# Sigmoid attention and a mixture of experts: three instructions put elsewhere in the loop over row blocks, two weight loads on another queue

## The chip, the cores and the metric

The kernel runs on one core of a Trainium2 chip. The metric is device time in microseconds (us), as the median of several runs. The core has a matrix engine (TensorE, PE in the profile; its weight loads are the row PEld), a vector engine (VectorE, DVE), a scalar engine (ScalarE, ACT), a general engine (GpSimd, POOL) and SyncE (SP), which here does little but start transfers. The engines run side by side, each through its own instructions in their order, and wait for each other by semaphores.

## What is computed

The reference, cut to what matters:

```python
# q, k, v: 8 batches x 12 heads x 448 positions x 64, float32
scores = q @ k^T / sqrt(64) - log(448)
attn = (1 / (1 + exp(-scores))) @ v
x = attn.transpose(0, 2, 1, 3).reshape(3584, 768)

# moe: w_skip 768, w_gate 768 x 8, w1 8 x 768 x 1024, w2 8 x 1024 x 768
out = x.copy()
do_compute = x @ w_skip > 0
xc = x[do_compute]
logits = xc @ w_gate
e_idx = argmax(logits)
gate_w = softmax(logits)[e_idx]
for e in range(8):                       # rows whose expert is e
    h = maximum(xc[e_idx == e] @ w1[e], 0)
    y[e_idx == e] = gate_w * (h @ w2[e])
out[do_compute] = xc + y
```

So a row either keeps its attention result, or gets a weighted two-layer network of one of eight experts added to it. Which rows go to which expert is known only once the attention is done.

## The kernel before

**Stages.** The attention runs over 48 pairs of heads and writes `x` to the output in memory. Beside it the rows are routed, and for each expert a list of records (row number and gate weight) is written to `lst`. Behind it stand two blocks of 128 rows of the expert with most rows, written out by hand, and then a loop over the blocks that are left, 14 in this run (L1565 and following). Each turn of that loop handles the rows of one block: gather them from memory, transpose them, multiply by the first weights (`ph`), apply the maximum and transpose (`pht`), multiply by the second weights (`py`), weigh the result, and add it to the rows in memory by a scatter.

**Exactness.** TensorE's fast float32 form (fp32r) keeps fewer bits, so each operand is split in two: a rounded high part `h` and the low part `l` that is left. Three products, high by high, high by low and low by high, give the result. For the weights these are `wh` and `wl` (from `raw`, the loaded weights), for the rows `xh` and `xl` (from `pxt`, the transposed rows), for the middle layer `hh` and `hl` (from `pht`).

**Four arms.** A table `slots`, worked out on the chip, says which kind each turn is. `block(i, False)` is a full block of 128 rows. `block(i, True)` is the splitting arm: a full block, the last for one expert's `wh` and `wl`, in which the next expert's `raw` weights are split into them as the products let go of them. `half(i)` and `few(i)` handle up to 64 and up to 32 rows of an expert straight from `raw`, in plain float32, and load the next expert's weights into `raw`. Every engine has the four arms in its program and jumps to the one that the table names, so a wait at the head of an arm must hold whichever arm ran before it; waits across arms are for counts that all arms make equal.

**What sets the order.** In an arm the order on each engine is that in which the code is written (`manual_schedule`). Ahead of the loop it is written too, but a scheduler may place instructions of the stretch up to L1257.

**Records.** `recs` holds three records for each partition: [0] the current block's, [1] the next one's, [2] the one after. `rn` is where GpSimd gathers the record after that. `advance()` (L1333 to L1339) moves [1] and [2] to [0] and [1] by way of `sv`, and casts the new [0]'s row number to the integer `rid`; with one piece for the splitting arm (one copy each way) and two for the others. `take_rec()` copies `rn` into [2] (L1343), at the head of the half and few arms and behind the first `hl` in the full and splitting ones.

**GpSimd in a block.** `fetch()` (L1280 and following) reads the next block's row numbers (`ri`, `rp[1]`), gathers its rows into `xn` (L564) and its record into `rn` (L414). `put()` (L1306 and following) reads the current block's row numbers from `rid` into `rp[0]` (L1308), looks at the weighed rows `ys` so that they are seen as done (`jk`), and scatters them with an addition (L574). In the splitting arm two of the eight low parts of the second weights, `wl2[6]` and `wl2[7]`, are subtracted on GpSimd (L1396), between `fetch()` and `put()`; two are done by VectorE ahead of the weighing and four behind `advance()`.

**Loads ahead of the loop.** The loop's first turn needs `raw` weights: first weights in four parts (`load_w1`) and second weights in four parts (`load_w2`). SyncE issues the four first parts and the second parts 0 and 1; all but the very first of these stand behind a wait for `done`, the last matmul of the blocks written out by hand. ScalarE issues the second parts 2 and 3, behind its own work on the first transposed rows (`xf`).

Of the kernel before, what the change touches and what calls it, by code (L numbers as in the profile page):

```python
# [15 lines left out]
ALU = mybir.AluOpType  # L16
# [7 lines left out]
def kernel(  # L24
# [11 lines left out]
    nc = tc.nc  # L36
# [3 lines left out]
    NE, _, FF = w1.shape  # L40
# [9 lines left out]
    NK2 = FF // P  # L50
# [51 lines left out]
    recs = const.tile([P, 3, REC], F32, name="recs")  # L102
    rn = const.tile([P, REC], F32, name="rn")
    nc.vector.memset(rn, 0.0)
    rid = const.tile([P, 3], I32, name="rid")
# [10 lines left out]
    wh2 = [wts.tile([P, DM], F32R, name=f"wh2_{i}") for i in range(NK2)]  # L116
    wl2 = [wts.tile([P, DM], F32R, name=f"wl2_{i}") for i in range(NK2)]
# [371 lines left out]
    def turn_x(x, h, px):  # L489
        for j in range(3):  # L490
            i = 3 * h + j
            nc.tensor.transpose(  # L492
                px[:, j * P : (j + 1) * P], x[:, i * P : (i + 1) * P], ident
            )
# [13 lines left out]
    def gemm1(h, part, xh, xl, ph, lag=False):  # L508

        kinds = ((xh, wh1), (xh, wl1), (xl, wh1))  # L510
        t = [(2 * j + 3 * (n == 2) if lag else 2 * n * NK1, n, j) for n in range(3) for j in range(NK1)]
        t.sort()
        for n in part:
            _, kind, j = t[n]
            a, w = kinds[kind]
            nc.tensor.matmul(  # L516
                ph[h],
                a[:, j * P : (j + 1) * P],
                w[j][h],
                start=(n == 0),  # L520
                stop=(n == len(t) - 1),
            )

    def relu(h, hs, ph):
        nc.scalar.activation(hs[:, h * H1 : (h + 1) * H1], ph[h], AF.Relu)  # L525

    def turn_h(h, hs, pt):
        for j in range(4):
            m = 4 * h + j
            nc.tensor.transpose(  # L530
                pt[:, j * P : (j + 1) * P], hs[:, m * P : (m + 1) * P], ident
            )

    def split_h(h, pt, hh, hl):
        nc.scalar.activation(hh[h], pt, AF.Copy)  # L535
        nc.vector.tensor_tensor(hl[h], pt, hh[h], op=ALU.subtract)  # L536

    def gemm2(j, hh, hl, py):
        h, m = divmod(j, 4)
        js = slice(m * P, (m + 1) * P)  # L540
        parts = [(n, o) for n in range(3) for o in range(2)]
        for n, o in parts:
            a, w = ((hh, wh2), (hh, wl2), (hl, wh2))[n]
            last = nc.tensor.matmul(  # L544
                half_y(py, o),
                a[h][:, js],
                w[j][:, o * H2 : (o + 1) * H2],
                start=(j == 0 and n == 0),
                stop=(j == NK2 - 1 and n == 2),
            )  # L550
        return last
# [493 lines left out]
    first_i = const.tile([P, 2], I32, name="first_i")  # L1045
# [48 lines left out]
    def whole_x(h, pieces):  # L1094
        for s in pieces:
            n = s.stop - s.start
            nc.scalar.activation(  # L1097
                xf[:, 3 * h + s.start : 3 * h + s.stop, :],
                pxt[h][:, s.start * P : s.stop * P].rearrange(
                    "p (j t) -> p j t", j=n  # L1100
                )[:, :, :MD],
                AF.Copy,
            )
# [98 lines left out]
    raw2 = [raw2g[j // 2][:, j % 2, :] for j in range(NK2)]  # L1202
# [15 lines left out]
            cond=nx[1],  # L1218
        )

    def load_w2(g, nx, queue=nc.sync):
        queue.dma_start(
            raw2g[g],
            w2[ds(nx[0], 1), g * 2 * P : (g + 1) * 2 * P, :].rearrange(
                "o (i p) f -> p (o i) f", p=P
            ),
            cond=nx[1],
        )

    def hi1(i, h):  # L1230
        nc.scalar.activation(wh1[i][h], raw1[i][h], AF.Copy)

    def lo1(i, h):
        nc.vector.tensor_tensor(wl1[i][h], raw1[i][h], wh1[i][h], op=ALU.subtract)

    def hi2(i):
        nc.scalar.activation(wh2[i], raw2[i], AF.Copy)

    def lo2(i):
        nc.vector.tensor_tensor(wl2[i], raw2[i], wh2[i], op=ALU.subtract)  # L1240

    dve, pool = nc.vector, nc.gpsimd
    ET = mybir.EngineType
    others = [e for e in mybir.ALL_ENGINES if e not in SP]
    kind_sp = nc.alloc_registers("kind", engines=SP)
# [2 lines left out]
    def look_ahead(col):  # L1248
        for reg, (j, most) in zip(
            (kind_sp, *names), ((TYP, SPLIT), (NXT, NE - 1), (HAS, 1))  # L1250
        ):
            nc.reg_mov(reg[ET.SP], entry(j, col, SP, most))

    def named():
# [4 lines left out]
    nx = (  # L1259
        nc.values_load(first_i[0:1, 1:2], engines=SP, min_val=0, max_val=NE - 1),  # L1260
        nc.values_load(first_i[0:1, 0:1], engines=SP, min_val=0, max_val=1),
    )

    nx_act = (
        nc.values_load(first_i[0:1, 1:2], engines=[ET.Activation], min_val=0, max_val=NE - 1),
        nc.values_load(first_i[0:1, 0:1], engines=[ET.Activation], min_val=0, max_val=1),
    )

    for n in range(4):
        load = load_w1(n % 2, n // 2, nx)  # L1270
        if n == 1:
# [5 lines left out]
            )  # L1277
        if n == 0:
            look_ahead(slice(2, 3))
    for g in range(4):  # L1280
        load_w2(g, nx if g < 2 else nx_act, nc.sync if g < 2 else nc.scalar)

    def fetch():


        pool.tensor_tensor(xn[:, 0:1], xn[:, 0:1], zf, op=ALU.add)
        pool.tensor_tensor(jk, rn[:, 0:2], rn[:, 0:2], op=ALU.add)
        pool.tensor_copy(ri, rn[:, 1:2])
        pool.tensor_tensor(rn[:, 0:1], rn[:, 0:1], zf, op=ALU.add)
        pool.tensor_tensor(rx, rix[:, 5:6], zero, op=ALU.add)  # L1290
        pool.tensor_tensor(rp[1], ri, zero, op=ALU.add)
        pool.tensor_tensor(rq, rp[1], zero, op=ALU.add)
        got = gather(xn, rp[1])

        tc.declare_no_dep(got.ins, group="put", across_iterations=True, reason="a token is in one block only")
        tc.add_to_no_dep_group("got", got.ins)
        gather_rec(rn, rx)
# [34 lines left out]
    def advance(pieces=2):  # L1332

        n = 2 // pieces
        for j in range(pieces):
            nc.vector.tensor_copy(sv[:, j * n : (j + 1) * n], recs[:, 1 + j * n : 1 + (j + 1) * n, 0:2])
        for j in range(pieces):
            nc.vector.tensor_copy(recs[:, j * n : (j + 1) * n, 0:2], sv[:, j * n : (j + 1) * n])
        nc.vector.tensor_copy(rid[:, 0:1], recs[:, 0, 1:2])  # L1339

    def take_rec():

        nc.vector.tensor_copy(recs[:, 2, 0:2], rn[:, 0:2])  # L1343

    def weigh_sum(y, p, gate):
        nc.vector.tensor_scalar(y, p, gate, None, op0=ALU.mult)

    def block(i, last):


        def split1(js, h):
            if last:
                for j in js:
                    hi1(j, h)
                for j in js:
                    lo1(j, h)

        look_ahead(ds(i + 3, 1))
        gemm1(0, range(G1), xh, xl, ph, last)
        relu(0, hs, ph)  # L1360
        split1(range(3), 0)
        gemm1(1, range(9), xh, xl, ph, last)
        turn_h(0, hs, pht[0])
        split_h(0, pht[0], hh, hl)
        take_rec()
        split1(range(3, NK1), 0)
        gemm1(1, range(9, G1), xh, xl, ph, last)
        relu(1, hs, ph)
        for h in range(2):
            turn_x(xn, h, pxt[h])  # L1370
        fetch()
        split1(range(3), 1)
        gemm2(0, hh, hl, py)
        turn_h(1, hs, pht[1])
        split_h(1, pht[1], hh, hl)
        split1(range(3, NK1), 1)
        if last:
            for h in range(2):
                whole_x(h, (slice(0, 3),))
            shift(dve)  # L1380
        else:
            ready_x()
        for j in range(1, NK2):
            gemm2(j, hh, hl, py)
        if last:
            for j in range(2):
                hi2(j)
            for h in range(2):
                hi_x(h, pxt[h], xh)
            for j in range(2, NK2 - 2):  # L1390
                hi2(j)
            for j in range(2):
                lo2(j)
            for j in range(NK2 - 2, NK2):
                dve.tensor_copy(wh2[j], raw2[j])
                pool.tensor_tensor(wl2[j], raw2[j], wh2[j], op=ALU.subtract)  # L1396
            for h in range(2):
                lo_x(h, pxt[h], xh, xl)
        else:
            shift(dve)  # L1400
        for o in range(2):
            rows = ys if last else yt
            weigh_sum(rows[:, o * H2 : (o + 1) * H2], half_y(py, o), recs[:, 0, 0:1])
        put(P, last)
        advance(1 if last else 2)
        if last:
            for j in range(2, NK2 - 2):
                lo2(j)

    def few(i):  # L1410

# [50 lines left out]
        for g in range(4):  # L1462
            load_w2(g, nx)
# [134 lines left out]
```

## Time and profile before

| what | value |
| --- | --- |
| time, median of 3 runs (lowest to highest) | 525.26 us (525.13 to 527.0) |
| the profiled execution's own time | 523.72 us |
| its span, first to last instruction | 521.8 us |
| granted TensorE clock, mean over the span | 0.992 of full speed |
| TensorE matmuls | 506.6 us busy, 97% of the span |
| VectorE | 298.0 us, 57% |
| ScalarE | 278.8 us, 53% |
| GpSimd | 266.6 us, 51% |
| loop over blocks | from 321.84 us of the span to its end |

The table is to be read so: times in the profile count from the start of the span, which is 1.9 us shorter than the execution's own time. An instruction's row in a timeline has its start, its length, its engine, the line, the operation with `output<-input`, the tile's shape, and in brackets how long the engine had waited ahead of it and for whom. "xN" at the end of a row stands for N such instructions one after another, with the length of all of them together.

### The profile page before, as it was taken

How to read it: one execution, taken by the hardware profiler on the slowest of the kernel's cores; microseconds unless marked ns; L12 is line 12 of the kernel's file. 1: busy time of each engine (PE TensorE's matmuls, PEld its weight loads, DVE VectorE, ACT ScalarE, POOL GpSimd, SP SyncE). 2: the span in 40 equal slices, each digit the busy share in tenths (PEclk: the TensorE clock that was granted, in tenths of full speed). 3: DMA queues.
4: the chain of work that ended last, by engine and by line, in shares of the span. 5: the costliest groups of instructions: out<-in, count | busy, mean ns of one | idle time of the engine just before them, and what ended most of it. 6: DMA issues, size and time to landing. Idle time of an engine off the chain costs nothing.

```text
span 521.8 us, 15390 instructions
## 1 busy us (share of the span) xinstructions
PE 506.6 (97%) x5033; PEld 341.5 (65%) x5034; DVE 298.0 (57%) x721; ACT 278.8 (53%) x481; POOL 266.6 (51%) x418
## 2 busy tenths in 40 slices
PE   8999999999999999999999999999999999999991
PEld 6875555545555446555455989948669797978790
DVE  4556856658668678587684952872223323249532
ACT  5776776767767667677674211942122323267221
POOL 4523553443557775766674332373333545456654
PEclk9999999999999999999999999999999999999996
DMA  8998887897989989999955017859393969696932
GB/s 210 214 248 187 174 178 160 171 179 174 202 187 239 234 193 206 206 217 219 197 117 119 11 42 241 336 169 360 98 355 139 329 234 346 237 348 214 361 121 47
DMA packets 140288, 107.21 MB, mean 205 GB/s; under 512 B 97099, under 2 KB 112731, under 8 KB 140240
## 3 DMA queue, kind: packets, MB, share of 16 engines
q1 hardware_dynamic: 133456, 96.09, 69.8%
q0 software_dynamic: 4576, 8.65, 6.9%
q10 hardware_dynamic: 2208, 1.83, 1.1%
q8 instruction: 30, 0.49, 0.4%
q14 instruction: 18, 0.15, 0.1%
HBM read 98.49 MB, written 17.56 MB: 222 GB/s over the span
## 4 chain that ended last, share of the span: by engine, by line
PE 95%; ACT 1%; DVE 1%; POOL 1%; issue 1%; DMA 1%; ACTq 0%; POOLq 0%; DVEq 0%
PE s L212 25%; PE pa L240 24%; PE py L544 11%; PE ph L516 11%; PE b_ph L516 3%; PE b_py L544 3%; PE py L1416 3%; PE ph L1416 3%; PE py L1485 2%; PE ph L1485 2%; PE pxt L492 2%; PE pl L280 2%; PE pht L530 1%; PE pg L297 1%; DMA kq_first<-in_q_dram 1%
## 5 line engine op out<-in xcount | busy, mean ns | idle before, releaser
L232 ACT ACTIVATE at<-s,bias 128x896 f32<-128x896 f32 (+1 forms) x191 | 173.8, 913 | 79.5 <-PE s L212 70.5
L212 PE MATMUL s<-x 64*64 64x448 f32 (+1 forms) x1528 | 170.2, 496 | 0.7 <-DVE x L194 0.7
L240 PE MATMUL pa<-at,v 64*64 64x448 f32 (+1 forms) x1536 | 168.5, 490 | 0.0
L176 POOL COPY kq<-kq 32x896 f32<-32x896 f32 (+1 forms) x96 | 87.7, 913 | 92.3 <-DMA kq<-in_q_dram 56.3
L212 PEld LDWEIGHTS s<-x 64*64 64x64 f32 x1528 | 83.9, 191 | 49.1 <-issue 25.2
L240 PEld LDWEIGHTS pa<-at,v 64*64 64x64 f32 x1536 | 65.6, 133 | 55.0 <-issue 45.7
L194 DVE STREAM_TRANSPOSE x<-kq 128x448 f32<-128x448 f32 x94 | 81.0, 936 | 4.4 <-PE pa L240 4.4
L250 DVE TENSOR_TENSOR xt<-xt,pa 128x448 f32<-128x448 f32 x48 | 29.8, 620 | 52.6 <-ACT xt L673 52.6
L414 POOL DMA_INDIRECT lst<-rec,idx x32 | 31.7, 990 | 17.8 <-DVE xt L250 5.7
L486 POOL TENSOR_TENSOR wl<-wr,wh 128x384 fp32r<-128x384 f32 (+1 forms) x28 | 31.2, 1124 | 12.8 <-DVE wh L485 8.3
L255 DVE STREAM_TRANSPOSE y<-xt 128x448 f32<-128x448 f32 x48 | 31.0, 645 | 5.8 <-DMA out_dram<-y 4.4
L574 POOL DMA_INDIRECT out_dram<-ys,rp x15 | 23.5, 1570 | 16.6 <-issue 8.4
L525 ACT ACTIVATE hs<-ph 128x512 f32<-128x512 f32 x14 | 8.4, 597 | 42.8 <-PE ph L516 34.8
L544 PE MATMUL py<-wh,hh 128*128 128x384 f32 x112 | 29.9, 348 | 0.0
L544 PE MATMUL py<-wh,hl 128*128 128x384 f32 x112 | 28.9, 339 | 0.5 <-DVE hl L536 0.5
L544 PE MATMUL py<-wl,hh 128*128 128x384 f32 x112 | 28.7, 337 | 0.0
L502 DVE TENSOR_TENSOR xl<-pxt,xh 128x384 fp32r<-128x384 f32 x30 | 15.3, 552 | 21.3 <-ACT xf L1097 20.8
L516 PE MATMUL ph<-wl,xh 128*128 128x512 f32 x84 | 26.6, 403 | 0.0
L536 DVE TENSOR_TENSOR hl<-pht,hh 128x512 fp32r<-128x512 f32 x14 | 9.7, 690 | 29.6 <-ACT hh L535 28.2
L673 ACT ACTIVATE xt<-pa 128x448 f32<-128x448 f32 x48 | 25.7, 535 | 0.8 <-PE pa L240 0.8
L516 PE MATMUL ph<-wh,xh 128*128 128x512 f32 x84 | 25.7, 403 | 0.0
L516 PE MATMUL ph<-wh,xl 128*128 128x512 f32 x84 | 24.5, 396 | 0.0
(279 smaller groups left out, 686.8 us busy)
## 6 DMA issues: line engine op xcount, KB each, us to landing
raw<-in_moe_w_dram SPq DMA_DIRECT2D x62, 768.0 KB
v<-in_v_dram SPq DMA_DIRECT2D x48, 256.0 KB
out_dram<-y SPq DMA_DIRECT2D x192, 56.0 KB
kq<-in_k_dram SPq DMA_DIRECT2D x46, 224.0 KB
kq<-in_q_dram SPq DMA_DIRECT2D x46, 224.0 KB
wr<-in_moe_w_dram SPq DMA_DIRECT2D x12, 256.0 KB
wr<-in_moe_w_dram SPq DMA_DIRECT2D x16, 192.0 KB
lst<-fill SPq DMA_DIRECT2D x4, 464.0 KB
```

What stands on the lines that cost most here:

```text
L176: nc.gpsimd.tensor_copy(a[BT:, :, :, :BT], a[:BT, :, :, BT:])
L194: nc.vector.transpose(xs[:, n].rearrange("p (r j) -> p j r", j=NJ), t.rearrange("p (j d) -> p j d", d=D)[:, :, :BT],)
L212: nc.tensor.matmul(sc[m * D : (m + 1) * D, j, : qs.stop - qs.start], xs[r, 0, first::NR7], xs[r, 1, qs], start=True, stop=True,)
L232: nc.scalar.activation(at[:, :, :n], sc[:, :, :n], AF.Sigmoid, bias=bias, scale=SCALE)
L240: nc.tensor.matmul(pa[j * D : (j + 1) * D, r, qs], vt[rs, j, r + c if c < 3 else 3 * (1 - r), :], at[rs, j, : qs.stop - qs.start], start=( ...
L250: nc.vector.tensor_tensor(x, x, pa[:, 1, :S], op=ALU.add)
L255: nc.vector.transpose(y, xts[b][:, hp, :])
L414: put = nc.gpsimd.indirect_dma_start(out=lst[:, :], out_offset=bass.IndirectOffsetOnAxis(ap=idx[:, c : c + 1], axis=0), in_=rec[:, c, :], ...
L486: nc.gpsimd.tensor_tensor(lo, r, hi, op=ALU.subtract)
L516: nc.tensor.matmul(ph[h], a[:, j * P : (j + 1) * P], w[j][h], start=(n == 0), stop=(n == len(t) - 1),)
L544: last = nc.tensor.matmul(half_y(py, o), a[h][:, js], w[j][:, o * H2 : (o + 1) * H2], start=(j == 0 and n == 0), stop=(j == NK2 - 1 and n ...
L1416: nc.tensor.matmul(dst[g * SM : (g + 1) * SM, :n], a, w, start=(j == 0), stop=(j == most - 1), tile_position=(0, g * SM),)
```

## The change

Three edits.

1. The cast of the row number (`rid`) leaves `advance()`, at the end of a block, and goes to `take_rec()`, behind the take of the record. GpSimd's `rp<-rid` in `put()` thereby waits for VectorE's cast of the same block, and the cast for GpSimd's read in the block before.
2. In the splitting arm GpSimd's two subtractions of low parts go from ahead of `put()` to the end of the arm, behind `advance()`. `lo2` gets an engine as its argument.
3. Ahead of the loop the second weights' parts 2 and 3 are issued by SyncE instead of ScalarE, right behind the first load and ahead of the wait for `done`. ScalarE's registers for them (`nx_act`) go.

```diff
-    def load_w2(g, nx, queue=nc.sync):
-        queue.dma_start(
+    def load_w2(g, nx):
+        nc.sync.dma_start(
...
-    def lo2(i):
-        nc.vector.tensor_tensor(wl2[i], raw2[i], wh2[i], op=ALU.subtract)
-
     dve, pool = nc.vector, nc.gpsimd
+
+    def lo2(i, eng=dve):
+        eng.tensor_tensor(wl2[i], raw2[i], wh2[i], op=ALU.subtract)
+
...
-    nx_act = (
-        nc.values_load(first_i[0:1, 1:2], engines=[ET.Activation], min_val=0, max_val=NE - 1),
-        nc.values_load(first_i[0:1, 0:1], engines=[ET.Activation], min_val=0, max_val=1),
     )
...
         if n == 0:
             look_ahead(slice(2, 3))
-    for g in range(4):
-        load_w2(g, nx if g < 2 else nx_act, nc.sync if g < 2 else nc.scalar)
+            for g in range(2, 4):
+                load_w2(g, nx)
+    for g in range(2):
+        load_w2(g, nx)
...
         for j in range(pieces):
             nc.vector.tensor_copy(recs[:, j * n : (j + 1) * n, 0:2], sv[:, j * n : (j + 1) * n])
+
+    def take_rec():
+
+        nc.vector.tensor_copy(recs[:, 2, 0:2], rn[:, 0:2])
         nc.vector.tensor_copy(rid[:, 0:1], recs[:, 0, 1:2])
-
-    def take_rec():
-
-        nc.vector.tensor_copy(recs[:, 2, 0:2], rn[:, 0:2])
...
             for j in range(NK2 - 2, NK2):
                 dve.tensor_copy(wh2[j], raw2[j])
-                pool.tensor_tensor(wl2[j], raw2[j], wh2[j], op=ALU.subtract)
...
         put(P, last)
         advance(1 if last else 2)
         if last:
-            for j in range(2, NK2 - 2):
-                lo2(j)
+            for j in range(2, NK2):
+                lo2(j, dve if j < NK2 - 2 else pool)
```

**GpSimd, the splitting arm.** The rows below are GpSimd's instructions from the record gather of `fetch()` to the scatter of `put()`, before. A row has the line, the operation and `output<-input` with the shape; `wl_6` and `wl_7` are the low parts 6 and 7, `REGISTER_ALU` a register step that keeps a wait's count.

```order
L1115 DMA rn<-lst,rx 128x16
L1396 TENSOR_TENSOR wl_6_130<-raw_3_4371,wh_6_122 128x768
L1396 REGISTER_ALU
L1396 TENSOR_TENSOR wl_7_131<-raw_3_4371,wh_7_123 128x768
L1308 TENSOR_TENSOR rp_4354<-rid,zero 128x1
L1309 REGISTER_ALU
L1309 TENSOR_TENSOR rs<-rp_4354,zero 128x1
L1314 REGISTER_ALU
L1314 TENSOR_TENSOR jk<-ys 128x2
L574 DMA out_dram<-ys,rp_4354 3584x768
```

And of the changed kernel, from the read of the row numbers to the arm's end:

```order
L1306 TENSOR_TENSOR rp_4354<-rid,zero 128x1
L1307 REGISTER_ALU
L1307 TENSOR_TENSOR rs<-rp_4354,zero 128x1
L1312 REGISTER_ALU
L1312 TENSOR_TENSOR jk<-ys 128x2
L574 DMA out_dram<-ys,rp_4354 3584x768
L1242 REGISTER_ALU
L1242 TENSOR_TENSOR wl_6_130<-raw_3_4371,wh_6_122 128x768
L1242 REGISTER_ALU
L1242 TENSOR_TENSOR wl_7_131<-raw_3_4371,wh_7_123 128x768
```

The two subtractions stood ahead of the store and stand behind it now; what comes next on GpSimd is `fetch()` of the following turn.

**VectorE, from a block's end to the next one's head.** Before, the end of the few arm, with `advance()` and its cast (`ISA` is a wait by itself):

```order
L1336 COPY sv<-recs 128x2 x2
L1338 REGISTER_ALU
L1338 COPY recs<-sv 128x2
L1338 REGISTER_ALU
L1338 COPY recs<-sv 128x2
L1339 ISA
L1339 CAST rid<-recs 128x1
L1555 UNCONDITIONAL_BRANCH
```

And the difference in the splitting arm, behind its first `hl`:

```order
 L536 REGISTER_ALU
 L536 TENSOR_TENSOR hl_4352<-pht,hh_4349 128x512
-L1343 COPY recs<-rn 128x2
+L1340 COPY recs<-rn 128x2
+L1341 ISA
+L1341 CAST rid<-recs 128x1
 L1234 REGISTER_ALU
 L1234 TENSOR_TENSOR wl_3_0_110<-raw_0_1_4348,wh_3_0_98 128x512
```

The cast with its wait has left the end of the block and stands behind the take of the record, in the full and splitting arms thereby behind `hl`; what is queued behind it there is the fourth low part of the first weights.

**SyncE ahead of the loop.** Before, from the first weight load on (`raw_0_0` to `raw_1_1` are the first weights' parts, `raw_0` to `raw_3` the second's):

```order
L1213 DMA raw_0_0_4347<-in_moe_w_dram 128x3x512
L1213 ISA
L1213 DMA raw_0_1_4348<-in_moe_w_dram 128x3x512
L1213 ISA
L1213 DMA raw_1_0_4365<-in_moe_w_dram 128x3x512
L1213 ISA
L1213 DMA raw_1_1_4366<-in_moe_w_dram 128x3x512
L1222 ISA
L1222 DMA raw_0_4367<-in_moe_w_dram 128x2x768
L1222 ISA
L1222 DMA raw_1_4368<-in_moe_w_dram 128x2x768
```

And now, from the same load on:

```order
L1213 DMA raw_0_0_4347<-in_moe_w_dram 128x3x512
L1222 ISA
L1222 DMA raw_2_4370<-in_moe_w_dram 128x2x768
L1222 ISA
L1222 DMA raw_3_4371<-in_moe_w_dram 128x2x768
L1213 ISA
L1213 DMA raw_0_1_4348<-in_moe_w_dram 128x3x512
```

Second parts 2 and 3 have come to this queue, behind the first load and ahead of the wait in front of `raw_0_1`; the rest follows as before.

## What it does to the time: the prediction

> **What bounds the kernel now.** I read the page's first two parts, then the chain of waits in order of time over the loop, and at each place where that chain leaves TensorE the timeline around it.
>
> ```profile
> span 521.8 us, 15390 instructions
> PE 506.6 (97%) x5033; PEld 341.5 (65%) x5034; DVE 298.0 (57%) x721; ACT 278.8 (53%) x481; POOL 266.6 (51%) x418
> ```
>
> TensorE is busy for 506.6 of 521.8 us, so only its few gaps can be won. The chain (columns: start, length, what) shows where they lie.
>
> ```profile
> 321.84 6.46 PE ph L516 x27
> ...
> 340.36 5.30 PE ph L1485 x24
> ...
> 452.10 2.76 PE ph L1416 x96
> ...
> 458.65 6.49 PE ph L516 x27
> ...
> 469.53 0.62 PE py L544 x2
> ...
> 477.96 2.76 PE ph L1416 x96
> ...
> 482.51 3.00 PE py L1416 x32
> 485.51 6.50 PE ph L516 x27
> ```
>
> The loop's 14 blocks can be told from the lines: L516 opens a full or splitting block, L1485 a half, L1416 a block for few rows. The first splitting block runs from 321.84 to 340.36, 18.52 us without a gap; the second from 458.65 to 477.96, 19.31 us. So the second loses 0.79 us, around 469.5, where TensorE waits for VectorE's `hl`. A block for few rows takes 458.65 - 452.10 = 6.55 us; the one behind the second split takes 485.51 - 477.96 = 7.55 us. It loses 1.00 us before its `py`. These two are the only gaps in the loop that the change can close: 1.79 us together, 0.34% of the time.
>
> **The first gap, and the moved cast.** The timeline at the second split's start:
>
> ```profile
> 463.66 1.66 ACT L1231 ACTIVATE wh<-raw 128x512 fp32r<-128x512 f32 x3
> 464.70 0.15 DVE L1339 CAST rid<-recs 128x1 int32<-128x1 f32 x1 [3.58 <-POOL rp L1308]
> 466.85 1.90 DVE L1234 TENSOR_TENSOR wl<-raw,wh 128x512 fp32r<-128x512 f32 x3 [2.00 <-PE ph L516]
> ```
>
> At the end of the block for few rows VectorE stands for 3.58 us before the row number cast, because GpSimd has not yet read the old numbers (its `rp` waits for the previous store to land). Only then does VectorE turn to the next block, and its first subtraction begins at 466.85, though ScalarE's high parts are there from 464.3 on (463.66 and a third of 1.66). `hl` stands behind three such subtractions. With the cast behind the take of the record, in the next block and behind `hl`, VectorE can start some 2.5 us sooner. I take this gap as closed: -0.79. Bounds: 0 if ScalarE, not VectorE, set `hl`, and -0.79 since the first split has no gap. The cast itself is not saved: 14 casts of 0.15 us stand elsewhere. Its new wait is for the `rp` of the block before; queued behind it are VectorE's second `hl` or its `xl`. In the case shown `rp` is past by 464.7 and the take comes behind `hl`, so behind 468.7 today (466.85 + 1.90), and it is satisfied. `rp` in turn now waits for this block's cast, whole steps earlier. In all other blocks the wait that goes is hidden already, since the chain there is TensorE alone: 0.
>
> **The second gap, and the moved subtractions.** Around the second split's end:
>
> ```profile
> 478.61 3.61 POOL L1396 TENSOR_TENSOR wl<-raw,wh 128x768 fp32r<-128x768 f32 x2 [3.39 <-DVE wh L1395]
> 480.63 1.63 DVE L1336 COPY sv<-recs 128x4 f32<-128x4 f32 x1
> 482.29 0.17 DVE L1338 COPY recs<-sv 128x4 f32<-128x4 f32 x1
> 482.80 3.56 DVE L1240 TENSOR_TENSOR wl<-raw,wh 128x768 fp32r<-128x768 f32 x4
> 483.33 1.92 POOL L574 DMA_INDIRECT out_dram<-ys,rp  x1 [0.55 <-issue]
> 485.50 0.91 POOL L1287 TENSOR_TENSOR jk<-rn 128x2 f32<-128x2 f32 x1
> 488.07 1.08 POOL L564 DMA_INDIRECT xn<-out_dram,rp  x1 [0.74 <-PE ph L516]
> 494.38 0.82 PE L492 MATMUL pxt<-ident,xn 128*128 128x128 f32 x6
> ```
>
> The view names ScalarE's `xh` as what `py` waited for at 482.51. I don't believe it: in the block before that,
>
> ```profile
> 455.81 2.84 PE L1416 MATMUL py<-raw,ht 128*32 128x384 f32 x32
> 456.14 0.87 ACT L498 ACTIVATE xh<-pxt 128x384 fp32r<-128x384 f32 x2
> 456.86 0.18 POOL L1286 TENSOR_TENSOR xn<-xn,zf 128x1 f32<-128x1 f32 x1 [0.19 <-PE py L1416]
> 458.76 1.08 POOL L564 DMA_INDIRECT xn<-out_dram,rp  x1 [0.75 <-PE py L1416]
> ```
>
> `py` starts at 455.81, ahead of `xh` at 456.14. What ends just before 482.51 is VectorE's `recs<-sv` (482.29 + 0.17 = 482.46); TensorE's wait is a count of VectorE's instructions, common to all arms, and in the splitting arm it reaches to this copy. The copy is late because `sv` before it took 1.63 us, where the copy back of the same numbers takes 0.17. It ends at 482.26, when GpSimd's subtractions do (478.61 + 3.61 = 482.22). With them behind the store, the copy falls to about 0.17 and this gap closes as well: -1.00. Bounds: 0 if `xh` were the cause, and -1.00.
>
> **What is late next.** The two subtractions, 3.61 us, now stand on GpSimd's queue ahead of the next block's fetch, whose gather brings `xn` for the full block at 485.51. This gather took, from issue to landing:
>
> ```profile
> DMA to landing us min/median/max: 6.1/6.1/6.1
> ```
>
> So it lands at 488.07 + 6.1 = 494.2, and TensorE transposes `xn` at 494.38: today it is just in time. If TensorE comes 1.79 us sooner it is ready at 492.6, and the gather alone decides. Its new time: `sv` marks the end of the weighing, 480.63 - 0.79 = 479.84. The store follows after a probe of `ys`, priced as the 0.18 us operation of L1286, and 0.55 of issue as now, at 480.6, and with its 1.92 holds GpSimd to 482.5. Alone the subtractions would end at 486.1. But VectorE's four subtractions (0.89 us each) then run from about 480.5 (482.80 is 2.17 behind the start of `sv`; 1.46 of these go) to 484.1. The row of `jk` shows what meets there: 0.91 us at 485.50, up to 486.41, the end of VectorE's last one (482.80 + 3.56 = 486.36), for an operation like the 0.18 us one of L1286 at 456.86. So GpSimd's first subtraction waits for the running one to end, at 483.2, and runs to 485.0; VectorE's last goes in between, to 485.9; the second ends at 487.7. From there the fetch needs 458.76 - 456.86 = 1.90 us to its gather: 489.6, landing at 495.7, and TensorE starts 0.2 later: 495.9 against 494.38, **+1.5**. This replaces the -1.79; the two don't add, and a VectorE that is late with `xl` meanwhile hides under the same wait. Bounds: no meeting at all and a store of 1.41 us as in the last block (the row below) give 482.0, 485.6, 487.5, 493.6 and so -0.6; two full waits of 0.89 (487.9) and one more in the fetch (`jk` at 0.91 in place of 0.18: 2.63) give 490.5, 496.6 and +2.4.
>
> The Trainium skill, SBUF — State Buffer, Who interferes with whom, says that a VectorE instruction with two SBUF inputs contends with a GpSimd instruction that reads SBUF, and that whichever starts first holds the shared ports to its end. The rows show only the short GpSimd operation that waits; by this rule VectorE's subtraction also waits for a long one, which gives the +1.5, and without it the sum would be -0.1.
>
> Behind the first split the same delay is covered:
>
> ```profile
> 350.27 1.08 POOL L564 DMA_INDIRECT xn<-out_dram,rp  x1 [0.75 <-PE py L1485]
> DMA to landing us min/median/max: 6.8/6.8/6.8
> 361.46 0.82 PE L492 MATMUL pxt<-ident,xn 128*128 128x128 f32 x6
> ```
>
> It lands at 357.1 for a use at 361.46; 4.4 us of slack against at most 2.4, or 3.2 where TensorE gains no 0.79 as that split has no gap.
>
> **The loads ahead of the loop.**
>
> ```profile
> 312.82 1.00 POOL L564 DMA_INDIRECT xc<-out_dram,rid  x1 [0.30 <-issue]
> DMA to landing us min/median/max: 3.9/3.9/3.9
> 317.87 0.82 PE L492 MATMUL pxt<-ident,xc 128*128 128x128 f32 x6
> ```
>
> ScalarE issued the third and fourth second weights behind its work on these transposes; SyncE now does so right behind its first load, ahead of this gather, since what they wait for is past. Two weight loads then run beside the gather of `xc`, which today lands at 312.82 + 3.9 = 316.7, 1.15 us ahead of its use. Nothing is won in return: the first split has no gap. The gathers of `xn`, most of them beside such loads, give the price:
>
> ```profile
> DMA to landing us min/median/max: 3.4/5.4/6.8
> ```
>
> Unchanged it costs 0; at 6.8 it lands at 319.6, and with 0.2 to the start TensorE loses 319.8 - 317.87 = 1.95. I take the median, 5.4: 318.2, start 318.4, **+0.55**. The Trainium skill, DMA: Bandwidth & Descriptors, Queues, rings and completion order, says that each DMA engine takes turns between the queues that have work; by that the gather would get half the rate for its whole length, and the sum would stay near this; no run here shows it for `xc`. The two other loads of SyncE keep their place behind `done`, and what ScalarE saves in issues hid beside TensorE.
>
> **The tail.** The last store is on the chain:
>
> ```profile
> 515.66 1.41 POOL out_dram L574
> ```
>
> Its `rp` has one more wait, long satisfied, for a register step: below 0.05, and 0 in the sum.
>
> **Sum.** +1.5 + 0.55 = +2.05. The profiled execution took 523.72 us, 521.8 of it span; it would take 525.8. The median of the runs shown is 525.26, 1.54 above the profiled one, so I predict 525.26 + 2.05 = **527.3 us**.
>
> **Rivals.**
> - *The gains stay* (22%). GpSimd and VectorE don't meet and the gather lands in time; for it speaks that the store leaves nearly 3 us sooner, against it that 3.61 us stand before the fetch. From -1.79 with nothing late to -0.6 by the low bound above; at -0.6 524.7.
> - *The load holds back the first rows* (15%), slower beyond doubt: SyncE's two loads delay `xc` to a landing after 6.8 us, +1.95, and with +1.5 that is 528.7; with both upper ends, +4.35, 529.6. It decides as soon as `xc` takes over 317.87 - 0.2 - 312.82 = 4.85 us. For it speaks the load's place directly ahead, against it that a first load already ran beside the gather at 3.9.
> - *Nothing of it reaches TensorE* (8%): `hl` and `py` wait as before since ScalarE is the bound, and the gather comes no later: 525.3.
>
> My own case has the other 55%, with its range -0.1 to +3.5: 525.2 to 528.8.
>
> **How the numbers follow.** The range leaves out the part of the first rival below -0.9 and the top of the second: 524.4 to 529.4. A measurement of this kernel tells about 0.5% (2.6 us) from no change, so faster means below 522.6, which no bound reaches: 0.03 for what I don't see. Slower means above 527.9: nearly all of the second rival and some fifth of my own case, 0.25. The rest, 0.72, is the same.
>
> **What would show it.** In the changed kernel's timeline: the cast at the head of the blocks and no wait for `rp` at their ends; the second splitting block near 18.5 us and the block behind it near 6.55; `sv` there at 0.2 us; the two GpSimd subtractions behind the store, longer than 1.8 us each or with a gap; then the gather near 489.6 less the entry's shift, and TensorE idle before `pxt` in the following full block. At the entry, `xc` landing later than 3.9 us and a gap before its transposes. I am wrong if that gather is issued before 488, or lands in under 5 us, or if TensorE stands at `hl` or `py` as before.

## The result, and the profile after

The changed kernel takes 531.12 us (median of 6 runs, 529.31 to 532.26) against 525.19 us before (6 runs beside them, 524.62 to 527.0): a ratio of 1.0105, 95% interval 1.0088 to 1.0123. It is slower by 5.9 us, where 2.05 was forecast, and lies above the range. The profiled execution took 531.16 us.

The page's first two parts, after:

```profile
span 529.2 us, 15413 instructions
PE 510.3 (96%) x5033; PEld 343.6 (65%) x5034; DVE 302.6 (57%) x721; ACT 278.5 (53%) x481; POOL 270.6 (51%) x418
```

The span grew by 7.4 us, but TensorE is also *busy* for 3.7 us more with the same 5033 matmuls. Waits alone can't do that: some matmuls ran slower. The chain of waits, after (lines above L1250 have moved by two or three):

```profile
310.84 0.45 PE b_pht L814 x4
...
313.80 7.24 DMA xc<-out_dram,rid
321.08 0.88 PE pxt L492 x6
...
325.10 6.46 PE ph L516 x27
...
462.05 6.53 PE ph L516 x27
...
490.38 0.17 DVE wl L1242
...
491.25 0.16 DVE recs L1340
491.47 7.94 PE ph L516 x21
...
511.46 2.76 PE ph L1413 x96
```

and the row of the chain before that answers to the first:

```profile
309.85 0.44 PE b_pht L814 x4
```

Read by stages, each against the same stage before:
- Ahead of 310 us the changed kernel is 0.99 us later. That is the attention, whose length differs from run to run: in the profiles of this study its end (the first product of the blocks by hand) lies between 282.94 and 285.16, and the profile of before is the earliest of all. It is no part of the change.
- At the entry 325.10 - 321.84 = 3.26, less these 0.99: **+2.27**. The gather of `xc` takes 7.24 us from issue to landing, and is on the chain.
- Up to the second splitting block +0.14, in that block 18.52 in place of 19.31: **-0.79**. In the block for few rows behind it 6.55 in place of 7.55: **-1.00**. Both gaps have closed.
- In the full block behind that, from the start of its first product to that of the next block's, 24.28 in place of 18.56: **+5.72**. From there on nothing differs.

The timeline at that place shows what the chain's odd rows (VectorE's `wl`, then `recs`, then TensorE) mean:

```profile
480.57 2.83 PE L1413 MATMUL ph<-raw,xf 128*32 128x128 f32 x96
483.13 0.16 DVE L1334 COPY sv<-recs 128x4 f32<-128x4 f32 x1
483.52 7.80 DVE L1242 TENSOR_TENSOR wl<-raw,wh 128x768 fp32r<-128x768 f32 x4
485.44 4.20 POOL L1242 TENSOR_TENSOR wl<-raw,wh 128x768 fp32r<-128x768 f32 x2
487.12 1.66 PE L516 MATMUL ph<-wh,xh 128*128 128x512 f32 x6
489.76 1.59 POOL L1285 TENSOR_TENSOR jk<-rn 128x2 f32<-128x2 f32 x1
491.25 0.16 DVE L1340 COPY recs<-rn 128x2 f32<-128x2 f32 x1
491.46 2.93 PE L516 MATMUL ph<-wl,xh 128*128 128x512 f32 x6 [2.69 <-DVE rid L1341]
493.04 1.07 POOL L564 DMA_INDIRECT xn<-out_dram,rp  x1 [0.75 <-PE ph L516]
494.19 2.76 PE L516 MATMUL ph<-wh,xl 128*128 128x512 f32 x6
496.75 1.96 PE L516 MATMUL ph<-wh,xh 128*128 128x512 f32 x6
501.79 0.82 PE L492 MATMUL pxt<-ident,xn 128*128 128x128 f32 x6
```

`sv` takes 0.16 us, as foreseen. VectorE's four subtractions take 7.80 us, 3.56 before. Behind them on its queue stands the take of the record, and TensorE starts its first low-part product 0.05 us after that take (491.25 + 0.16 = 491.41), having stood for 2.69 us. Then three groups of six products take 2.93, 2.76 and 1.96 us, where 1.66 is the first group's and 1.56 the rule: about 3 us more.

How the 7.80 us are shared out, from the answer on the tile `wl` (duration in ns: least, median, most):

```profile
L1242 DVE TENSOR_TENSOR wl<-raw,wh x4: 945/956/5189, 483.5 to 490.4; 128x768 fp32r<-128x768 f32 x4
L1242 POOL TENSOR_TENSOR wl<-raw,wh x2: 2412/2413/2414, 485.4 to 487.2; 128x768 fp32r<-128x768 f32 x2
```

Three of VectorE's are as ever; the third took 5.19 us, from 485.27 to 490.46, and so ended 0.82 us, about the length of one alone, behind the end of GpSimd's second (485.44 + 4.20 = 489.64). The two engines do not take turns here. And the windows (length; busy time of PE, PEld, DVE, ACT, POOL; granted clock; DMA share; GB/s) show the slow products:

```profile
487.38:490.79 3.41, 1.40 (x6) 0.79 (x5) 3.41 (x2) 0.22 (x1) 3.41 (x5) 1.00 1.03 282
490.79:494.21 3.42, 2.75 (x7) 2.17 (x8) 3.25 (x12) 0.93 (x2) 2.41 (x7) 0.50 1.05 319
494.21:497.62 3.41, 3.41 (x10) 2.64 (x9) 0.24 (x3) 0.55 (x1) 2.75 (x8) 0.50 1.03 412
497.62:501.03 3.41, 3.41 (x18) 2.82 (x17) 0.42 (x1) 0.64 (x2) 1.41 (x1) 1.00 1.04 390
```

TensorE's granted clock was full up to 490.79, near the end of the idle time, half for 6.83 us from there, and full again from 497.62 on.

### The profile page after: what moved, and what is told of

Its sections match the earlier page's. It is cut to its first block, busy times and chain, and to the rows that moved or that the text cites. A ratio compares the mean times of both kernels' runs of the same rounds, so it can differ in the third digit from the quotient of the medians.

```text
span 529.2 us, 15413 instructions
## 1 busy us (share of the span) xinstructions
PE 510.3 (96%) x5033; PEld 343.6 (65%) x5034; DVE 302.6 (57%) x721; ACT 278.5 (53%) x481; POOL 270.6 (51%) x418
## 4 chain that ended last, share of the span: by engine, by line
PE 93%; issue 2%; DMA 1%; DVE 1%; POOL 1%; ACT 1%; DVEq 0%; POOLq 0%; ACTq 0%
PE s L212 25%; PE pa L240 24%; PE ph L516 12%; PE py L544 11%; PE b_ph L516 3%; PE b_py L544 2%; PE py L1413 2%; PE ph L1413 2%; PE py L1482 2%; PE ph L1482 2%; PE pxt L492 2%; PE pl L280 2%; DMA xc<-out_dram,rid 1%; PE pht L530 1%; PE idle L627 1%
## 5 line engine op out<-in xcount | busy, mean ns | idle before, releaser
L240 PEld LDWEIGHTS pa<-at,v 64*64 64x64 f32 x1536 | 67.0, 133 | 54.8 <-issue 47.7
L516 PE MATMUL ph<-wl,xh 128*128 128x512 f32 x84 | 27.9, 422 | 2.7 <-DVE rid L1341 2.7
L516 PE MATMUL ph<-wh,xl 128*128 128x512 f32 x84 | 25.7, 412 | 0.0
```

The costliest lines, as they stand in the source:

```text
L240: nc.tensor.matmul(pa[j * D : (j + 1) * D, r, qs], vt[rs, j, r + c if c < 3 else 3 * (1 - r), :], at[rs, j, : qs.stop - qs.start], start=( ...
L516: nc.tensor.matmul(ph[h], a[:, j * P : (j + 1) * P], w[j][h], start=(n == 0), stop=(n == len(t) - 1),)
```

## The experiments

All times are medians beside runs of the kernel before; the ratio's 95% interval is in brackets. The table has, for one profiled execution of each, three stretches of TensorE's work taken from the starts of its products: from the first product of the blocks by hand to the first transposes of `xc` (entry), the block for few rows ahead of the second split with that split (few + split), the block for few rows behind it (few), and the full block that follows.

| kernel | time, beside before | ratio | entry | few + split | few | full |
| --- | --- | --- | --- | --- | --- | --- |
| before | | | 34.94 | 25.86 | 7.55 | 18.56 |
| all three edits | 531.12, 525.19 | 1.0105 [1.0088, 1.0123] | 37.15 | 25.24 | 6.55 | 24.28 |
| e1_cast | 524.9, 525.36 | 0.9988 [0.9976, 1.0] | 34.97 | 25.22 | 7.39 | 18.52 |
| e2_subs | 528.46, 525.36 | 1.0064 [1.0043, 1.0084] | 34.95 | 25.65 | 6.55 | 22.17 |
| e3_loads | 527.88, 525.36 | 1.0055 [1.0035, 1.0074] | 36.99 | 25.84 | 7.53 | 18.52 |
| e4_no_loads | 528.12, 525.36 | 1.0046 [1.0029, 1.0063] | 34.94 | 25.22 | 6.55 | 22.90 |
| e5_subs_vector | 524.9, 525.32 | 0.9989 [0.9972, 1.0005] | 34.95 | 25.09 | 7.59 | 18.56 |
| e6_one_behind | 526.51, 525.32 | 1.0015 [0.9995, 1.0035] | 34.93 | 25.09 | 6.73 | 20.64 |
| e7_one_ahead | 525.76, 525.32 | 0.9999 [0.9982, 1.0016] | 34.97 | 25.13 | 8.21 | 18.56 |
| e8_one_load | 527.13, 525.32 | 1.0024 [1.0006, 1.0042] | 36.09 | 25.93 | 7.53 | 18.55 |
| e9_reduce | 524.7, 525.5 | 0.9983 [0.9966, 1.0] | 34.92 | 25.09 | 7.38 | 18.56 |
| e10_cast_again | 524.4, 525.5 | 0.9982 [0.9967, 0.9997] | 34.97 | 25.09 | 7.39 | 18.53 |
| e11_loads_behind | 525.45, 525.5 | 0.9996 [0.9981, 1.0011] | 34.96 | 25.36 | 7.52 | 18.54 |
| e12_all_again | 530.98, 525.19 | 1.0093 [1.0069, 1.0118] | 37.11 | 25.11 | 6.60 | 22.88 |

### Each edit by itself

The theory after the reading: three effects that add, one of each edit. The rivals: the loss belongs to another edit, or to the gather of `xn` as predicted.

**e1_cast**: the kernel before with the first edit (`rid` cast in `take_rec`).

> The cast alone. My theory: the second splitting block falls from 19.31 to about 18.6 us and the rest stays, so -0.7 us against the kernel before. Rival: the cast's new wait for GpSimd, with VectorE's next work queued behind it, is what costs time in the changed kernel; then this kernel is slower by some 3 to 6 us by itself, with TensorE idle in the full block behind the second split.

0.5 us faster at the edge of the interval, few + split 0.64 shorter, the full block unchanged. The cast's wait costs nothing; its rival falls.

**e2_subs**: the second edit (`lo2` on GpSimd behind `advance`).

> The moved subtractions alone. My theory: the block for few rows behind the second split falls by 1.0 us to 6.55; in the full block behind it VectorE's third low part is held for some 5 us beside GpSimd's two, the take of the record comes that much later, and TensorE idles about 2.7 us ahead of its first product with a low part; +1.7 us where TensorE's clock stays, up to +4.7 where it falls to half for some 6 us after the idle time. Rival (the step as predicted): the gather of xn decides, TensorE idles about 1.5 us before pxt and not before; +1.5 us at most. Rival of the cast: no loss here, -1.0 us.

+3.1 us. The timeline:

```profile
490.23 0.15 DVE L1344 COPY recs<-rn 128x2 f32<-128x2 f32 x1
490.44 1.67 PE L516 MATMUL ph<-wl,xh 128*128 128x512 f32 x6 [3.16 <-DVE recs L1344]
492.01 1.07 POOL L564 DMA_INDIRECT xn<-out_dram,rp  x1 [0.73 <-PE ph L516]
498.14 0.84 PE L492 MATMUL pxt<-ident,xn 128*128 128x128 f32 x6
```

There is no cast at this place in this kernel, and TensorE starts 0.06 us after the take all the same: so it is the take that it waits for, not the cast which the changed kernel's row names. The semaphore records of the trace fit: the product waits for VectorE's counter, and the take raises this counter by a number, where its neighbours count one. The product needs low parts of first weights, which only a splitting arm makes, so a block for few rows would give all of these counts at once, with its take; the counts themselves are not in the trace. In this execution the products keep 1.67 us (no fall of the clock), and the full block is 3.6 us longer: 3.3 at the take (the first low-part product starts 490.44 - 485.61 = 4.83 us into the block, 1.51 before) and the rest behind it, 0.16 of this at `pxt`, 6.13 us after the gather's issue. So there are two waits, one behind the other. The first is where TensorE stands; the second, the gather that I had predicted, still ends last by some 0.2 us and sets the sum where the clock holds.

**e3_loads**: the third edit.

> The two loads alone. My theory: the gather of xc lands about 7.2 us after its issue in place of 3.9, TensorE waits for it some 2.0 us ahead of the first transposes, and nothing is won elsewhere: +2.0 us. Rival: the longer gather of the changed kernel was one execution's chance, and the price is the 0.55 us that I predicted or nothing.

+2.5 us, and the wait stands where expected:

```profile
314.94 1.00 POOL L564 DMA_INDIRECT xc<-out_dram,rid  x1 [0.30 <-issue]
322.07 0.87 PE L492 MATMUL pxt<-ident,xc 128*128 128x128 f32 x6 [1.88 <-DMA xc<-out_dram,rid]
```

**e4_no_loads**: the first and second edit.

> Cast and subtractions together, loads as before. My theory: the three edits add: -0.7 -1.0 +2.7 and up to 3.0 more where the clock falls, so +1.0 to +4.0 us, and the entry as in the kernel before. Rival: loads and subtractions need each other (the loads' shift moves the meeting of VectorE and GpSimd), then this one is not slower than the kernel before.

+2.8 us. With e3's +2.5 that makes +5.3; all three together have +5.9, within the intervals. The edits add, and need nothing of each other.

### What holds VectorE

**e5_subs_vector**: the cast, and both subtractions on VectorE.

```diff
-                pool.tensor_tensor(wl2[j], raw2[j], wh2[j], op=ALU.subtract)
...
-            for j in range(2, NK2 - 2):
-                lo2(j)
+            for j in range(2, NK2):
+                lo2(j, dve)
```

> The cast, and both subtractions behind the store on VectorE instead of GpSimd; loads as before. My theory (GpSimd's two hold VectorE's third for 5.2 us): nothing is held any more; VectorE's six take 6 x 0.89 = 5.3 us in place of 7.8, the take comes about 2.4 us sooner than with GpSimd, and TensorE's 2.7 us of idle time in the full block shrink to about 0.3, with no fall of the clock; -1.6 + 0.3 = -1.3 us against the kernel before. Rival (VectorE is late simply because the block for few rows is 1 us shorter and the fetch comes behind): most of the loss stays, 0 to +1.

```profile
480.90 5.30 DVE L1242 TENSOR_TENSOR wl<-raw,wh 128x768 fp32r<-128x768 f32 x6
482.11 3.50 PE L1416 MATMUL py<-raw,ht 128*32 128x384 f32 x32 [0.31 <-ACT ht L1444]
486.12 0.16 DVE L1343 COPY recs<-rn 128x2 f32<-128x2 f32 x1
487.04 1.56 PE L516 MATMUL ph<-wl,xh 128*128 128x512 f32 x6
```

Six subtractions in 5.30 us, 0.88 each: without GpSimd beside them none is held, the take comes at 486.12, and the full block is back at 18.56. The main theory holds. The time is only 0.4 us below that of before, though, since the block for few rows lost again what it had won (7.59): its `py` takes 3.50 us. I had not expected this. TensorE's count for `py` is reckoned from the arm's end; with two more VectorE instructions there it no longer falls on the copy to `recs` but on the second of the six subtractions: in the trace TensorE's wait for VectorE's counter inside `py` ends at 482.77, 0.04 us behind the end of that subtraction.

**e6_one_behind**: one of the two on GpSimd behind the store, the other on VectorE.

> The cast, one subtraction behind the store on GpSimd and the other on VectorE; loads as before. My theory: VectorE's third is held for one GpSimd subtraction only, some 2.4 us less than for two, but VectorE has one more of 0.9 us: the take comes some 1 to 1.5 us sooner than with both on GpSimd, TensorE idles 1.2 to 2.0 us; between 0 and +0.5 us. Rival (VectorE and GpSimd alternate, so that a VectorE instruction waits for one GpSimd instruction at most): held about as long as with two, less than 2.5 us, and idle time much as now.

```profile
481.16 6.87 DVE L1242 TENSOR_TENSOR wl<-raw,wh 128x768 fp32r<-128x768 f32 x5
483.08 2.39 POOL L1242 TENSOR_TENSOR wl<-raw,wh 128x768 fp32r<-128x768 f32 x1
488.17 1.66 PE L516 MATMUL ph<-wl,xh 128*128 128x512 f32 x6 [1.56 <-DVE rid L1344]
489.74 1.07 POOL L564 DMA_INDIRECT xn<-out_dram,rp  x1 [0.74 <-PE ph L516]
495.93 0.84 PE L492 MATMUL pxt<-ident,xn 128*128 128x128 f32 x6
```

Five take 6.87, which is 2.4 more than 5 x 0.89; with two of GpSimd's the four took 4.2 more. One GpSimd subtraction holds VectorE for its length, two for both: turns would have given the same hold twice. The idle time is 1.56 as expected, and the gather is then late by another 0.2 us at `pxt`, 6.19 us after its issue. The stages of this execution add up to +0.5 (-0.77, -0.82 and +2.08), the top of what was expected. The median is +1.2, with an interval from -0.3 to +1.8 that holds +0.5; what the rest of it would be isn't shown.

**e7_one_ahead**: one of the two on GpSimd in the old place, the other on VectorE behind `advance`.

> The cast, one subtraction on GpSimd in its old place ahead of the store and the other on VectorE behind advance; loads as before. My theory: GpSimd is done before the copy to sv, so both gaps close (-0.6 and -1.0), and VectorE's five have nothing of GpSimd's beside them but the short ones of the fetch; the take comes ahead of TensorE's use; -1.5 us, TensorE's full block at 18.55. Rival: the copy is still held, by the one subtraction; then -0.6.

A miss: no change, and the block for few rows at 8.21.

```profile
479.17 1.83 POOL L1242 TENSOR_TENSOR wl<-raw,wh 128x768 fp32r<-128x768 f32 x1 [2.01 <-DVE wh L1396]
479.37 2.04 DVE L1396 CAST wh<-raw 128x768 fp32r<-128x768 f32 x1 [0.44 <-PE py L544]
483.12 0.84 PE L492 MATMUL pxt<-ident,xn 128*128 128x128 f32 x6 [0.77 <-DVE ys L1347]
```

GpSimd now starts between VectorE's two casts of `wh` and holds the second: 2.04 us for what takes 0.56. The hold was not removed but moved. By itself it doesn't give the 8.21: in e1_cast the second cast is held for 2.04 us too, and `ys` begins 3.00 us into the block for few rows, 3.01 here, yet that block takes 7.39. The difference is what TensorE waits for. In e1_cast its transposes wait for `xl` (0.24 us), here for `ys` (0.77), and `py` takes 3.54 in place of 3.00. As in e5_subs_vector, one more VectorE instruction at the arm's end shifts where TensorE's count falls; the trace's wait inside `py` ends 0.04 us behind the first of the five subtractions.

**e9_reduce**: the cast; the copies to `sv` and back as reductions, GpSimd's work where it was.

```diff
+        if pieces == 1:
+            V.tensor_reduce(sv, recs[:, 1:3, 0:2].unsqueeze(3), axis=AX.X, op=ALU.max)
+            V.tensor_reduce(recs[:, 0:2, 0:2], sv.unsqueeze(3), axis=AX.X, op=ALU.max)
+            return
```

> The cast; GpSimd's two subtractions in their old place ahead of the store; in the splitting arm the copies to sv and back to recs become reductions over an axis of length one on the same engine. My theory: what holds the copy for 1.6 us is the port that it shares with GpSimd, and a reduction doesn't take it: sv at about 0.2 us, the block for few rows near 6.55, and GpSimd free of VectorE's work later; then the gather of xn, issued some 0.5 us sooner at most, is what is late next by up to 1 us: -0.7 to -1.6 us in all. Rival: the copy waits for GpSimd for another reason (a semaphore), and the reduction starts no sooner: -0.6 as with the cast alone.

```profile
477.62 2.05 DVE L1399 CAST wh<-raw 128x768 fp32r<-128x768 f32 x1 [0.44 <-PE py L544]
479.81 1.82 POOL L1400 TENSOR_TENSOR wl<-raw,wh 128x768 fp32r<-128x768 f32 x1 [0.57 <-DVE wh L1399]
481.57 0.14 DVE L1336 TENSOR_REDUCE sv<-recs 128x4 f32<-128x4 f32 x1
```

No better than the cast alone. The reduction takes 0.14 us, but it comes only when GpSimd is as good as done (479.81 + 1.82 = 481.63), since the second cast was held as in e1_cast and e7_one_ahead. Whether a reduction can run beside GpSimd stays open.

### The loads

**e8_one_load**: the kernel before, one of the two loads ahead of SyncE's wait, the other last.

> The kernel before with one of the two second weight loads ahead of the wait on SyncE, the other behind it as the last. My theory (the gather of xc shares the DMA engines with the loads for as long as they last): landing between 3.9 and 7.2, near 5.5, TensorE waits some 0.4 us; +0.4 us. Rival (any load issued ahead of the gather costs it the full delay, or the second one alone does): 7.2 and +2.0, or 3.9 and 0.

```profile
315.04 6.17 DMA xc<-out_dram,rid
321.25 0.87 PE L492 MATMUL pxt<-ident,xc 128*128 128x128 f32 x6 [0.97 <-DMA xc<-out_dram,rid]
```

Landing after 3.9 us with no such load, 6.2 with one, 7.2 with two. The price comes by degrees, as the theory has it, but the first load costs more than half of it. +1.8 us in time where +0.4 was expected; 1.15 of these stand at the entry, and the interval reaches down to 0.3.

**e11_loads_behind**: both loads on SyncE, behind its other loads.

> The kernel before with the two second weight loads on SyncE, but behind its other loads and so behind the wait for the last product of the blocks by hand. My theory: the place ahead of the gather costs, not the queue: the gather of xc lands in about 3.9 us, no wait ahead of the first transposes; 0 us, unless the later loads are missed in the first splitting block. Rival: SyncE's queue or ScalarE's freed time is what matters, then +2 us here as well.

Entry 34.96, time unchanged. The place ahead of the gather costs; the queue does not.

### The spread

**e10_cast_again**: e1_cast once more.

> The cast alone, once more beside the others of this call: the second splitting block near 18.5, the block for few rows behind it near 7.4, -0.5 us as before. If the gain of the first time was chance, 0.

-1.1 us, interval clear of zero. The cast alone is a gain of 0.1 to 0.2%. None of the other kernels has a lower median, but e9_reduce, which has the cast too, can't be told from it.

**e12_all_again**: the changed kernel once more.

> The changed kernel once more, for its spread. My theory: the idle time ahead of the first low-part product stands in every execution, and in a part of them TensorE's granted clock falls behind it; so executions with a mean clock of 0.985 to 0.989 are 1.5 to 3 us longer than those with 0.992 and more, and the fastest are at +3.2 us or so over the kernel before (2.1 at the entry, -1.7 and +2.7 in the loop). Rival: the spread is that of the attention as in the kernel before, whose executions lie within 3.4 us too; then time and clock don't go together.

With the six runs of the result there are twelve. The six with a mean clock of 0.985 to 0.988 have spans of 529.2 to 530.5, the six with 0.991 or 0.992 spans of 527.3 to 529.1; so clock and time go together, some 1.5 us apart. The fastest, 527.3, is 4.1 us above the median span of the kernel before (523.2, eleven runs at 0.991 to 0.995), not 3.2: I had left out the gather's 0.2 behind the take, and the attention's spread may do the rest. A mean clock of 0.991 doesn't tell an execution without a fall from one with a short one: that of e4_no_loads in the profile has one, of 3.41 us, and 0.991.

In this execution the half clock stands also behind the entry's shorter wait. The first two windows are from this trace, the two behind them from that of e2_subs, where the clock stayed full:

```profile
319.46:322.87 3.41, 1.41 (x11) 1.09 (x10) 0.00 (x0) 0.03 (x1) 0.00 (x0) 1.00 0.87 343
322.87:326.28 3.41, 3.41 (x13) 3.41 (x12) 1.02 (x2) 1.54 (x8) 0.00 (x0) 0.50 0.04 9
PE pxt L492 <- DMA xc<-out_dram,rid: 2.0, 1, 2.0
485.66:489.08 3.42, 1.63 (x8) 1.00 (x6) 3.42 (x1) 1.15 (x2) 3.42 (x4) 1.00 1.00 313
489.08:492.49 3.41, 2.05 (x9) 1.68 (x10) 3.24 (x9) 0.00 (x0) 2.53 (x8) 1.00 1.06 291
```

The row between them is TensorE's wait at the entry. With 2.0 us of idle time there the clock fell in this execution, with the same wait in the first profile it did not; with 3.16 us in e2_subs it stayed full. What picks the executions can be read from the traces. In all fourteen the granted clock changes only at whole multiples of 3.41 us from the start of its record (ahead of its first fall it was full for 142 such stretches in the first profile, 93 here and, up to its end, 151 in e2_subs), and a fall lasts one stretch or two. It came behind stretches in which TensorE was busy for 1.40 us (first profile), 1.04 (e4_no_loads), 1.41 and 0.97 (here). It did not come behind those with 1.63 and 2.05 (e2_subs), 1.84 (e6_one_behind) or, at the entry, 2.33 and 2.46 in the first profile, where the edge of a stretch cut the same wait in two. So the length of a wait doesn't decide alone, but how much of it falls into one stretch: 2.0 us were enough here, 1.8 were not. These are four falls, those behind the last product left out; no kernel was run that fills the idle time.

## Why the prediction was wrong

**The gains** were right in place and size: -0.79 at `hl` and -1.00 at `py` in the changed kernel's trace, as forecast.

**The gather of `xn`** came where it was forecast, but by luck. It was forecast for 489.6 in the time of before; it stands at 493.04 in a trace whose second split starts 462.05 - 458.65 = 3.40 later: 489.64. Two errors of 1.5 us cancel in this. GpSimd's second subtraction was to end at 487.7 and ended at 489.64 - 3.40 = 486.24; the fetch was to need 1.90 us from there to its gather and took 493.04 - 489.64 = 3.40, with `jk` at 1.59 us beside VectorE's late subtractions. With 6.1 us to its landing and 0.2 to the start that lets TensorE go on at 495.9, the forecast +1.5 for the loop. Two executions fit that: the runs of e4_no_loads with the highest mean clocks, 0.994 and 0.995 (3.41 us at half cost 0.003 of the mean), have spans of 525.2 and 524.9 us, 1.7 and 1.4 above the median span of the kernel before, measured beside them (523.5). No trace of both edits without a fall was taken.

**The clause** "a VectorE that is late with `xl` meanwhile hides under the same wait" was right in its sum and wrong in its mechanism. I let VectorE and GpSimd take turns and allowed VectorE 1.8 us (484.1 to 485.9); in fact GpSimd's two went through together, and VectorE's four took 4.2 us longer than alone. And what TensorE needs there first is not `xl`, for the third group of products, but the take of the record, for the second. Two rows of the timeline of before show how near that was:

```profile
486.28 0.16 DVE L1343 COPY recs<-rn 128x2 f32<-128x2 f32 x1
486.95 1.56 PE L516 MATMUL ph<-wl,xh 128*128 128x512 f32 x6
```

The take ended 0.5 us ahead of its use, a slack that I never priced because no row showed a wait there. The 2.69 us of idle time that came of it would still have hidden: TensorE would be at `pxt` by 492.6 + 2.69 = 495.3, ahead of 495.9.

The Trainium skill, SBUF — State Buffer, Who interferes with whom, says that the engine which starts first holds the shared ports for its whole instruction. The rows of e7_one_ahead agree: GpSimd's subtraction starts at 479.17, VectorE's cast at 479.37, and the cast ends at 481.41, behind GpSimd's end at 481.00. Those of the changed kernel don't: there VectorE's third subtraction starts at 485.27, GpSimd's first at 485.44, and it is VectorE's that is held, for both of GpSimd's. In this case the start by the trace doesn't tell who is held; why VectorE didn't go between the two stays open.

**The step that failed** in the loop is the sum itself: it counts a wait of TensorE by its length. Behind 2.69 us of idle time the products ran at half clock and lost (2.93 + 2.76 + 1.96) - 3 x 1.56 = 2.97 us more; 495.3 + 2.97 = 498.3 is where `pxt` stands (501.79 - 3.40 = 498.39), and the gather, in by then, decides nothing. That is a term of up to 3 us in some executions and none in others; no part of the prediction has it. The idle time that I did forecast, ahead of `pxt`, was no shorter (495.9 - 492.6 = 3.3), so idle time of this length should have had a price beyond its length, if not in every execution.

The Trainium skill, TensorE: Matmul & The Clock Gate, What's actually happening, has the clock halved after an idle window of about 3.4 us. Here waits of 2.0 and 2.7 us were enough in some executions, with TensorE busy for 1.4 us of the 3.41 ahead of the fall, so the measurement decides: shorter waits count.

**The entry** was the right mechanism with a wrong size, the rival that I gave 15%. I priced the gather of `xc` by the median of other gathers, 5.4 us; measured are 7.2 us, and about 2.0 us of wait against 0.55. My upper bound, 6.8, was too low as well: the longest of the other gathers is no bound for one that is issued directly behind two added loads.

Together: 1.5 for the loop and 2.1 for the entry make 3.6; what is left of 5.9, some 2.3, is about what the clock takes in a middling execution (1.6 us in that of e4, 3.0 in the first profile). This last share is a difference, not a measurement by itself.

## What to carry to other kernels

Before work is moved behind a store or to a block's end, list what is queued behind it on both engines that it meets, and the first instruction anywhere that waits for that, also where the present wait is zero; and where two engines hold each other, as VectorE and GpSimd do here, reckon with the sum of the long instructions that follow directly and not only with turns. A wait of TensorE of 2 us or more may cost up to twice its length, as in the first profile (2.69 us, and 2.97 behind it), so two losses that hide each other are not always worth the larger one alone. A transfer that lands just in time is a place not to issue others ahead of.

## What the runs showed of the hardware

- GpSimd's 128x768 subtraction takes 1.8 us alone and 2.4 us where VectorE's meets it; VectorE's waited for both of two that follow directly (0.95 us against 5.19), though by the trace it had started first.
- A cast of 128x768 on VectorE, 0.56 us, took 2.04 beside one such subtraction.
- A row gather lands in 3.9, 6.2 or 7.2 us with none, one or two more weight loads issued ahead of it.
- TensorE's granted clock changed only on a grid of 3.41 us. It fell to 0.50 for 3.41 or 6.83 us behind stretches of this grid with 0.97 to 1.41 us of busy time, and did not behind those with 1.63 us or more.
